# One step later for a copy, and a weight split moved into the first four tiles of a layer: a fused LSH-attention and mixture kernel

## The chip, the cores and the metric

The kernel runs on one core of one Trainium2 chip. The metric is the device time of one execution in microseconds (us), as the median over several runs. One of the executions was also recorded by the hardware profiler; every duration below comes from that recording.

## What is computed

The reference takes `q`, `k`, `v` of shape (2, 8, 768, 64): two batches, eight heads, 768 positions, 64 channels. Its core, with the hashing of rows to buckets in front of it, is:

```
mask   = q_bucket[:, :, :, None] == k_bucket[:, :, None, :]     # 6 sign bits of q @ proj and k @ proj
scores = where(mask, (q @ k^T) / 8, -1e9)
attn   = softmax(scores);  attn_out = attn @ v                   # (2, 8, 768, 64)
x      = attn_out laid out as (1536, 512)                        # heads side by side
out    = sum over 4 experts e of p[:, e] * (relu(x @ w1[e]) @ w2[e])
```

`w1` is (4, 512, 1024) and `w2` is (4, 1024, 512); `p` is the row-normalised `domain_probs`. All of it is held to the precision of float32, which the kernel reaches by splitting each operand into a rounded high part and a remainder ("hi" and "lo") and adding three products: hi times hi, hi times lo, lo times hi.

## The kernel before, in words

**Two batches, interleaved.** The attention of batch 0 runs first. Then the expert layers of batch 0 (function `moe`) run on TensorE while the attention of batch 1 is threaded between their tiles. Last come the expert layers of batch 1 (`moe_fast`). The order of all instructions is the program's own: each engine (TensorE = PE, VectorE = DVE, ScalarE = ACT, GpSimd = POOL, SyncE = SP, which issues all DMAs) takes its instructions strictly in the order in which the program writes them, and waits in place for whatever an instruction lacks. Buffers are freed by semaphores: a new tile in a pool with one buffer waits for the last reader of the old one, even where that reader is written later in the program, on another engine.

**The units of the expert layers.** There are 8 units per batch, one per half expert (512 hidden columns). In batch 0 a unit u has a first layer (lines 654 to 680: two halves s of 384 rows, four tiles f each, 12 matmuls per tile, lines 664 to 666) and a second layer (lines 620 to 643: six tiles t, 12 matmuls each, lines 627 to 629). ACT writes the rectified tile `hh` (line 671), DVE its remainder `hl` (line 672); for a second-layer tile DVE adds the result to `acc` (line 635). The tiles of PSUM for all of these rotate through four banks, which the attention's `ptps` and `pv` tiles share.

**The weights.** `load_w` (line 578) loads one 512 KB half of a weight matrix into one of two staging buffers `ws`. `split_w` (line 592) is a generator with four pieces per matrix: in a piece DVE casts 128x512 values to the high part (line 600) and POOL subtracts to get the low part (line 601); after pieces 2 and 4 the staging buffer is reloaded. The first weights of the next unit are split during the second layer, a piece after each of its first four tiles. The second-layer weights `w2hi`, `w2lo` of the unit are split during its own first layer, a piece whenever line 677 asks `sp2` for one. Before, that is after f = 1 and f = 3 of s = 0, and after f = 1 and f = 3 of s = 1. In the last unit of batch 0 (u = 7) the rest of the attention is written out before s = 1, and `x_ops` (lines 712 to 740), the preparation of the inputs of batch 1 on DVE, ACT and POOL, is written into s = 1.

**The attention as a pipeline.** `attention()` (line 502) runs over 96 steps i, one per head and tile of 128 rows; stage letters in the order "TXVSENRP" are written at each step, each for an earlier tile by its own lag. S computes scores on PE (lines 341, 343), DVE masks them, E is the exponential on ACT (line 364), N and R send reciprocals of the sums through memory (`row`, `rdb`), P prepares the next head. From head 9 on ("light") the transposed score tile of a pair of tiles, called a group g here, is made without PE:

```
elif op == "X":
    for lag, f in ((LAG_H, stage_h), (LAG_X, stage_x)):
        j = i - lag
        if 0 <= j < n and light(*seq[j][:2]) and j % G == G - 1:
            f(b, h, t // G)
```

`stage_x` (line 414, lag 3): DVE transposes 32x32 blocks into `t1`, SP writes `t1` to memory (`scr`, line 425), then reads it back rearranged into `px` with four DMAs (line 428). There is one `px` buffer. `stage_h` (line 434, `LAG_H`): for two halves, ACT copies `px` into the high part `pthi` (line 442), POOL forms `ptlo` (line 443). `stage_v` (line 447, lag 7): PE multiplies with v in two parts, part 0 with `pthi` at lag 7 and part 1 with `ptlo` at lag 8 (line 453). There are 21 such groups. Since j is odd, X(g+1) stands in the step in which H(g) stands before the change. How many steps of attention stand between two tiles of the expert layers is set by the numbers that the generators yield; neither edit changes one of these.

Of the kernel before, what the change touches and what calls it, by code (L numbers as in the profile page):

```python
# [39 lines left out]
LAG_VL = 7  # L40
DRAIN = 1000
LAG_X = 3
LAG_H = 5


@with_exitstack
def tile_lsh_attention__then__domain_moe(
# [454 lines left out]
    def attention():  # L502
# [3 lines left out]
        def do(op, i):  # L506
# [15 lines left out]
# [3 lines that stand above are left out]
# [67 lines left out]
    def split_w(g, i):  # L592
        n = ("w1", "w2")[i]
        hi = wp.tile([P, KD, HALF], F32R, tag=n + "hi", name=n + "hi")
        lo = wp.tile([P, KD, HALF], F32R, tag=n + "lo", name=n + "lo")
        wts[g, i] = (hi, lo)
        for c in range(0, KD, WC):
            t = staged.pop((g, i, c))
            for o in range(WC):
                nc.vector.tensor_copy(hi[:, c + o], t[:, o])  # L600
                nc.gpsimd.tensor_tensor(  # L601
                    out=lo[:, c + o], in0=t[:, o], in1=hi[:, c + o].bitcast(F32), op=ALU.subtract
                )
                if o == WC - 1:
                    load_w()
                yield
# [3 lines left out]
    def moe_ps():  # L610
        return one("mps")

    def second_layer(b, u, first_u, hs, w2):
        e = u // (F // HALF)
        nxt = first_u + u + 1
        w2hi, w2lo = w2
        more = nxt < B * NU
        fast = nxt >= NU
        sp = (split_w1_fast(nxt) if fast else split_w(nxt, 0)) if more else iter(())
        for s in range(NS - 1, -1, -1) if b else range(NS):  # L620
            for t in range(TS):
                tt = s * TS + t
                ts = slice(t * P, (t + 1) * P)
                ps = moe_ps()
                for f in range(FC):
                    hh, hl = hs[s, f]
                    nc.tensor.matmul(ps, hh[:, ts], w2hi[:, f], start=f == 0, stop=False)  # L627
                    nc.tensor.matmul(ps, hh[:, ts], w2lo[:, f], start=False, stop=False)  # L628
                    nc.tensor.matmul(ps, hl[:, ts], w2hi[:, f], start=False, stop=f == FC - 1)  # L629
                pcol = pe[:, b, tt, e : e + 1]  # L630
                if u == 0:
                    accs[b, tt] = ap_.tile([P, DM], F32, tag=f"acc{tt}", name="acc")
                    nc.vector.tensor_scalar(out=accs[b, tt], in0=ps, scalar1=pcol, scalar2=None, op0=ALU.mult)
                else:
                    nc.vector.scalar_tensor_tensor(  # L635
                        out=accs[b, tt], in0=ps, scalar=pcol, in1=accs[b, tt], op0=ALU.mult, op1=ALU.add
                    )
                if u == NU - 1:
                    nc.sync.dma_start(
                        out=out[b * S : (b + 1) * S, :].rearrange("(p c) d -> c p d", c=NT)[tt], in_=accs[b, tt]  # L640
                    )
                next(sp, 0)
                yield 2600
        for _ in sp:
            pass

    def moe(b, first_u):
        for u in range(NU):
            w1hi, w1lo = wts.pop((first_u + u, 0))
            sp2 = split_w(first_u + u, 1) if first_u + u else iter(())  # L650
            hs = {}
            nxt = first_u + u + 1
            xo = None
            for s in range(NS):
                if nxt == NU and s == 1:
                    while next(att, None) is not None:
                        pass
                    xo = x_ops()
                sl = slice(s * SB, (s + 1) * SB)
                for f in range(FC):  # L660
                    fs = slice(f * P, (f + 1) * P)
                    ps = moe_ps()
                    for kk in range(KD):
                        nc.tensor.matmul(ps[:, :SB], w1hi[:, kk, fs], xhi[b, kk][:, sl], start=kk == 0, stop=False)  # L664
                        nc.tensor.matmul(ps[:, :SB], w1hi[:, kk, fs], xlo[b, kk][:, sl], start=False, stop=False)  # L665
                        nc.tensor.matmul(  # L666
                            ps[:, :SB], w1lo[:, kk, fs], xhi[b, kk][:, sl], start=False, stop=kk == KD - 1
                        )
                    hh = hp.tile([P, SB], F32R, tag=f"hh{f}", name="hh")
                    hl = hp.tile([P, SB], F32R, tag=f"hl{f}", name="hl")  # L670
                    nc.scalar.activation(hh, ps[:, :SB], ACTF.Relu)  # L671
                    nc.vector.scalar_tensor_tensor(  # L672
                        out=hl, in0=ps[:, :SB], scalar=0.0, in1=hh.bitcast(F32), op0=ALU.max, op1=ALU.subtract
                    )
                    hs[s, f] = (hh, hl)
                    if f % 2 == 1:
                        next(sp2, 0)
                    yield 1960
                    if xo is not None and (s, f) >= (1, 1):
                        next(xo, 0)  # L680
            for _ in xo or ():
                pass
            yield from second_layer(b, u, first_u, hs, wts.pop((first_u + u, 1)))
# [28 lines left out]
    def x_ops():  # L712
        pair_in("b11", ((xp, "xe0"),))
        pair_in("t1", ((xp, "xe1"),))
        t1 = combine(b12, b11, ALU.subtract)
        put_hi("b11", b11)
        put_hi("t1", t1)
        put_lo("b11", b11, nc.gpsimd)
        put_lo("t1", t1, nc.gpsimd)
        pair_in("b21", ((stk, "q1"), (stk, "al")))  # L720
        pair_in("b22", ((stk, "q1"), (stk, "al")))
        pair_in("t2", ((stk, "ah"), (stk, "k2")))
        pair_in("t3", ((stk, "ah"), (stk, "k2")))
        pair_in("t4", ((ex, "t1"),))
        t2 = combine(b22, t1, ALU.subtract)
        put_hi("b21", b21)
        t4 = combine(t2, b21, ALU.subtract)
        put_hi("t2", t2)
        put_lo("b21", b21, nc.gpsimd)
        yield  # L730
        t3 = combine(b22, b12, ALU.subtract)
        put_lo("t2", t2, nc.vector)
        put_hi("b22", b22)
        put_hi("t4", t4)
        put_lo("b22", b22, nc.gpsimd)
        yield
        put_hi("t3", t3)
        put_lo("t4", t4, nc.vector)
        put_lo("t3", t3, nc.gpsimd)
        yield  # L740
# [135 lines left out]
    with tc.manual_schedule():  # L876
# [25 lines left out]
        for b in range(B):  # L902
            dm = da = 0.0
            for c in (moe_fast if b else moe)(b, b * NU):
                dm += c
                while da < dm * ATT_PACE * n_att / n_moe:
                    x = next(att, None)
                    if x is None:
                        break
                    da += x  # L910
            if b == 0:
                for _ in att:
                    pass
# [28 lines left out]
```

## Time and profile before

| | us |
|---|---|
| median of 3 runs (784.24 to 785.15) | 784.28 |
| the profiled execution, its time | 785.92 |
| its span, first to last instruction | 784.2 |
| PE busy in the span | 743.6 |
| DVE, ACT, POOL busy | 507.0, 362.1, 339.8 |

How to read it: the profiled execution's time is 1.7 us longer than its span, and 1.6 us longer than the median. PE is busy in 95% of the span, and no other engine in more than 65%. Busy time of matmuls is modelled and overlaps, so the distance between starts is the surer measure of what a matmul costs. The granted clock of PE has two levels, 1.2 and 2.4 GHz, shown as 0.5 and 1.0.

### The profile page before, as it was taken

What the parts mean: (1) busy time and instruction counts of PE and PEld (TensorE: products, weight loads), DVE (VectorE), ACT (ScalarE), POOL (GpSimd) and SP (SyncE); (2) the same over time, 40 slices, a digit from 0 to 9 for tenths busy, and PEclk for the clock granted to TensorE, in tenths of its full rate; (3) what the DMA queues carried; (4) which work ended last, traced back from release to release, by engine and by line L of the source; (5) the groups of instructions that cost most, each with busy time, mean ns of one, the idle gap of its engine ahead of it and who ended that gap; (6) DMA issues with size and microseconds to landing.
All of it is one profiled execution on the core that took longest, in us unless ns stands there. A gap on an engine that the chain in (4) does not pass through costs nothing. (4 is left out here: it accounts for less than half of the span.)

```text
span 784.2 us, 11424 instructions
## 1 busy us (share of the span) xinstructions
PE 743.6 (95%) x4090; PEld 673.4 (86%) x4090; DVE 507.0 (65%) x957; ACT 362.1 (46%) x731; POOL 339.8 (43%) x290
## 2 busy tenths in 40 slices
PE   7899999998999979999998999789999999999998
PEld 5889989996988969989897898669889889898896
DVE  5799999945565557655755433766585675765853
ACT  5899999742434343625345130414343352343430
POOL 1232442613466446554665552653342342433420
PEclk9999999999999989999998999989999999999999
DMA  4544644433767666667756612041130212211302
GB/s 101 150 107 117 141 98 115 113 93 117 215 191 216 187 183 199 185 210 193 217 182 192 200 39 80 28 147 68 54 101 34 81 55 81 81 54 54 101 8 80
DMA packets 71953, 95.49 MB, mean 122 GB/s; under 512 B 31396, under 2 KB 47268, under 8 KB 71896
## 3 DMA queue, kind: packets, MB, share of 16 engines
q1 hardware_dynamic: 71896, 94.76, 41.7%
q8 instruction: 32, 0.52, 0.3%
q14 instruction: 25, 0.20, 0.1%
HBM read 62.68 MB, written 19.71 MB: 105 GB/s over the span
## 5 line engine op out<-in xcount | busy, mean ns | idle before, releaser
L627 PE MATMUL mps<-w2hi,hh 128*128 128x512 f32 x384 | 153.4, 399 | 15.9 <-DVE w2hi L600 12.4
L628 PE MATMUL mps<-w2lo,hh 128*128 128x512 f32 x384 | 152.1, 396 | 3.9 <-POOL w2lo L601 3.9
L629 PE MATMUL mps<-w2hi,hl 128*128 128x512 f32 x384 | 152.2, 396 | 0.0
L635 DVE SCALAR_TENSOR_TENSOR acc<-mps,pe,acc 128x512 f32<-128x512 f32 x84 | 62.8, 748 | 78.1 <-PE mps L629 77.1
L443 POOL TENSOR_TENSOR ptlo<-px,pthi 128x768 fp32r<-128x768 f32 x42 | 77.1, 1856 | 61.6 <-ACT pthi L442 60.9
L627 PEld LDWEIGHTS mps<-w2hi,hh 128*128 128x128 f32 x384 | 72.9, 190 | 33.9 <-issue 8.1
L803 POOL TENSOR_TENSOR w2lo<-ws,w2hi 128x512 fp32r<-128x512 f32 x32 | 45.8, 1452 | 120.3 <-ACT w2hi L802 120.3
L348 DVE TENSOR_SCALAR_CACHE_REDUCE p<-sps 128x768 f32<-128x768 f32 x96 | 90.7, 945 | 4.8 <-PE sps L343 4.4
L664 PE MATMUL mps<-xs,w1hi 128*128 128x384 f32 x256 | 87.8, 343 | 3.9 <-DVE hl L672 3.9
L672 DVE SCALAR_TENSOR_TENSOR hl<-mps,hh 128x384 fp32r<-128x384 f32 x64 | 35.6, 556 | 86.1 <-ACT hh L671 85.8
L364 ACT ACTIVATE p<-p,nb 128x768 f32<-128x768 f32 x96 | 89.5, 932 | 2.4 <-DVE p L348 1.8
L628 PEld LDWEIGHTS mps<-w2lo,hh 128*128 128x128 f32 x384 | 73.1, 190 | 20.1 <-POOL w2lo L601 6.6
L629 PEld LDWEIGHTS mps<-w2hi,hl 128*128 128x128 f32 x384 | 73.0, 190 | 17.6 <-DVE hl L832 2.4
L666 PE MATMUL mps<-xs,w1lo 128*128 128x384 f32 x256 | 86.8, 339 | 0.0
L665 PE MATMUL mps<-xs,w1hi 128*128 128x384 f32 x256 | 86.8, 339 | 0.0
L442 ACT ACTIVATE pthi<-px 128x768 fp32r<-128x768 f32 x42 | 33.2, 838 | 97.5 <-DMA px<-scr 97.5
L671 ACT ACTIVATE hh<-mps 128x384 fp32r<-128x384 f32 x64 | 30.9, 488 | 81.3 <-PE mps L666 81.1
L601 POOL TENSOR_TENSOR w1lo<-ws,w1hi 128x512 fp32r<-128x512 f32 x32 | 41.6, 1302 | 60.1 <-DVE w1hi L600 45.5
L601 POOL TENSOR_TENSOR w2lo<-ws,w2hi 128x512 fp32r<-128x512 f32 x32 | 42.4, 1329 | 50.5 <-DVE w2hi L600 26.0
L409 DVE TENSOR_TENSOR ptlo<-ptps,pthi 128x384 fp32r<-128x384 f32 x108 | 54.6, 547 | 8.4 <-ACT pthi L408 8.1
L343 PE MATMUL sps<-k,al 76*128 76x384 f32 x192 | 50.6, 344 | 3.6 <-POOL vv L302 2.6
L341 PE MATMUL sps<-ah,q 128*128 128x384 f32 x192 | 50.9, 345 | 2.3 <-DVE p L348 0.9
(134 smaller groups left out, 1567.4 us busy)
## 6 DMA issues: line engine op xcount, KB each, us to landing
ws<-in_moe_w_dram SPq DMA_DIRECT2D x64, 512.0 KB
scr<-t SPq DMA_DIRECT2D x21, 768.0 KB
px<-scr SPq DMA_DIRECT2D x84, 192.0 KB
q<-ah SPq DMA_DIRECT2D x30, 192.0 KB
tv<-in_v_dram SPq DMA_DIRECT2D x16, 192.0 KB
rdb<-row SPq DMA_DIRECT2D x48, 64.0 KB
out_dram<-acc SPq DMA_DIRECT2D x12, 256.0 KB
tqk<-in_q_dram SPq DMA_DIRECT2D x15, 192.0 KB
```

Source lines behind the costliest of these rows:

```text
L348: nc.vector.tensor_scalar(out=two(pt), in0=ps[:, :, :NH], scalar1=MASKED, scalar2=MASKED, op0=ALU.min, op1=ALU.min, accum_out=nb,)
L364: nc.scalar.activation(pt, pt, ACTF.Exp, bias=nb, scale=-1.0, accum_out=dens[b, h, g][:, o : o + 1])
L409: nc.vector.tensor_tensor(out=ol, in0=src, in1=oh.bitcast(F32), op=ALU.subtract)
L443: nc.gpsimd.tensor_tensor(out=fl[:, sl], in0=px[:, sl], in1=fh[:, sl].bitcast(F32), op=ALU.subtract)
L601: nc.gpsimd.tensor_tensor(out=lo[:, c + o], in0=t[:, o], in1=hi[:, c + o].bitcast(F32), op=ALU.subtract)
L627: nc.tensor.matmul(ps, hh[:, ts], w2hi[:, f], start=f == 0, stop=False)
L628: nc.tensor.matmul(ps, hh[:, ts], w2lo[:, f], start=False, stop=False)
L629: nc.tensor.matmul(ps, hl[:, ts], w2hi[:, f], start=False, stop=f == FC - 1)
L635: nc.vector.scalar_tensor_tensor(out=accs[b, tt], in0=ps, scalar=pcol, in1=accs[b, tt], op0=ALU.mult, op1=ALU.add)
L664: nc.tensor.matmul(ps[:, :SB], w1hi[:, kk, fs], xhi[b, kk][:, sl], start=kk == 0, stop=False)
L665: nc.tensor.matmul(ps[:, :SB], w1hi[:, kk, fs], xlo[b, kk][:, sl], start=False, stop=False)
L666: nc.tensor.matmul(ps[:, :SB], w1lo[:, kk, fs], xhi[b, kk][:, sl], start=False, stop=kk == KD - 1)
```

## The change

Two edits. The lag of `stage_h` goes from 5 to 6 steps: ACT's copy of `px` and POOL's subtraction are written one attention step later, after the X of the next group instead of before it, and one step before the first matmul that reads `pthi` instead of two. And a piece of the split of `w2` is written after each of the four tiles of s = 0, none in s = 1. The reload of the staging buffers moves with the pieces. It holds for units 1 to 7 of batch 0; unit 0's `w2` is split earlier, and `moe_fast` has its own split.

```diff
-LAG_H = 5
+LAG_H = 6
...
                     hs[s, f] = (hh, hl)
-                    if f % 2 == 1:
+                    if s == 0:
                         next(sp2, 0)
                     yield 1960
```

## Rows read from the trace of the kernel before

**Rows 1.** The page, busy time by engine (us, share of the span, instructions).
```profile
PE 743.6 (95%) x4090; PEld 673.4 (86%) x4090; DVE 507.0 (65%) x957; ACT 362.1 (46%) x731; POOL 339.8 (43%) x290
```

**Rows 2.** Busy time by stage, PE alone: stretch, length, busy, granted clock, DMA share, GB/s.
```profile
273.32:303.95 30.63, 25.49 (x122) 0.89 0.70 196
...
400.00:429.01 29.01, 25.60 (x140) 0.88 0.56 166
...
501.89:529.24 27.35, 18.58 (x73) 0.81 0.33 105
...
543.90:560.55 16.65, 16.65 (x73) 1.00 0.29 95
```

**Rows 3.** Who waited for whom, PE: total us, times, longest.
```profile
PE mps L627 <- DVE w2hi L600: 12.4, 3, 7.6
PE mps L628 <- POOL w2lo L601: 3.9, 5, 1.1
...
PE hps L275 <- DVE al L264: 3.1, 5, 1.5
```

**Rows 4.** Timeline, unit 7, end of first layer: start, length, engine, what, [idle before].
```profile
502.23 2.50 DVE L706 TENSOR_TENSOR xc<-xc,xraw 128x768 f32<-128x768 f32 x1
...
510.08 1.55 DVE L600 CAST w2hi<-ws 128x512 fp32r<-128x512 f32 x1
...
511.78 0.76 PE L627 MATMUL mps<-w2hi,hh 128*128 128x512 f32 x1 [7.64 <-DVE w2hi L600]
```

**Rows 5.** Timeline, PE, second layer of unit 2.
```profile
275.23 0.39 PE L629 MATMUL mps<-w2hi,hl 128*128 128x512 f32 x1
280.20 0.80 PE L627 MATMUL mps<-w2hi,hh 128*128 128x512 f32 x1 [4.59 <-DVE w2hi L600]
...
284.85 0.39 PE L627 MATMUL mps<-w2hi,hh 128*128 128x512 f32 x1
```

**Rows 6.** Timeline, ACT and DVE, the same stretch of unit 2.
```profile
275.37 1.58 ACT L442 ACTIVATE pthi<-px 128x768 fp32r<-128x768 f32 x2 [6.67 <-DMA px<-scr]
...
277.36 0.56 DVE L672 SCALAR_TENSOR_TENSOR hl<-mps,hh 128x384 fp32r<-128x384 f32 x1 [6.58 <-ACT hh L671]
...
279.18 0.97 DVE L600 CAST w2hi<-ws 128x512 fp32r<-128x512 f32 x1
```

**Rows 7.** Timeline, ACT and PE, first layer of unit 5.
```profile
415.97 1.57 ACT L442 ACTIVATE pthi<-px 128x768 fp32r<-128x768 f32 x2 [7.10 <-DMA px<-scr]
...
418.56 0.69 PE L664 MATMUL mps<-xs,w1hi 128*128 128x384 f32 x1 [3.41 <-DVE hl L672]
...
422.57 1.49 PE L453 MATMUL pv<-pthi,vv 128*128 128x256 f32 x6
```

**Rows 8.** Who waited for whom, ACT and SP, stretch 186 to 455.
```profile
ACT pthi L442 <- DMA px<-scr: 97.5, 18, 11.8
...
SPq L428 <- DMA scr<-t: 77.1, 21, 6.3
...
SPq L428 <- POOL ptlo L443: 0.9, 2, 0.8
```

**Rows 9.** Timeline, the DMA queue of SP, groups 4 and 5.
```profile
240.38 1.75 SPq L428 DMA_DIRECT2D px<-scr  x4
...
257.03 1.76 SPq L428 DMA_DIRECT2D px<-scr  x4
```

**Rows 10.** Timeline, ACT and POOL, group 5.
```profile
262.65 1.58 ACT L442 ACTIVATE pthi<-px 128x768 fp32r<-128x768 f32 x2 [3.13 <-DMA px<-scr]
...
263.58 3.84 POOL L443 TENSOR_TENSOR ptlo<-px,pthi 128x768 fp32r<-128x768 f32 x2 [5.41 <-ACT pthi L442]
```

**Rows 11.** Timeline, PE, the product with v: group 3 part 1, group 4 part 1, group 5 part 0.
```profile
252.27 0.88 PE L453 MATMUL pv<-ptlo,vv 128*128 128x256 f32 x6
...
261.45 0.88 PE L453 MATMUL pv<-ptlo,vv 128*128 128x256 f32 x6
...
267.10 0.88 PE L453 MATMUL pv<-pthi,vv 128*128 128x256 f32 x6
```

## The prediction

> **What bounds the kernel now.** I read the page first: PE is busy in 95% of the span, no other engine in more than 65% [rows 1]. So the time can fall only by what PE idles, or runs at its lower clock, and those have to be found stage by stage. The view of busy time by stage, cut at the starts of the first and second layers, shows where: the second layers of batch 1 take 16.65 us with PE never idle at the full clock, while three stages of batch 0 stand out by idle time and a granted clock under 1.00: the second layer of unit 2, the first of unit 5 and the second of unit 7 [rows 2]. The list of waits then names what ended the idle time: `w2hi` three times for 12.4 us in all, `w2lo` five times for 3.9, the head preparation's `al` [rows 3], and in unit 5 `hl`, 3.41 at once [rows 7].
>
> The timelines show why each was late. In unit 7 the fourth `w2hi` cast is the last thing on DVE behind `x_ops`, whose additions take up to 2.50; it ends at 511.6, and PE has waited 7.64 for it [rows 4]. In unit 2 the fourth cast stands behind `hl`, `hl` behind `hh`, and ACT could not do `hh` because it sat 6.67 us in front of `pthi`, waiting for `px` to land [rows 6]. Unit 5 is the same chain without the cast: ACT idle 7.10 for `px`, so `hh` and `hl` late, so no free PSUM bank [rows 7]. ACT spends 97.5 us, in 18 waits, at that instruction [rows 8]. Most of it cost PE nothing.
>
> Behind `px` stands SP: every `px` read waited for `scr` to land, 77.1 us in 21 waits, and only 0.9 us for POOL's `ptlo` to free the single `px` buffer [rows 8]. I expect that balance to turn.
>
> **Part one, the split of w2.** It removes and adds no instruction: 28 casts, 28 subtractions and 14 reloads in seven units stand earlier, in unit 7 before `x_ops`.
> - *Unit 7.* The stage takes 27.35 and the undisturbed one 16.65 [rows 2]: 10.7 us, with the half clock after the stall in it. What is late next is DVE: `x_ops` without the cast ends near 511, then come the six additions to `acc` and the mixes for batch 1. PE without the stall reaches its fifth tile at 501.9 + 4 x 2.78 = 513.0 (16.65 / 6 for a tile), when the first tile's bank has to be free, about 512.5 by DVE's queue. It fits without margin. I take 10.7 and keep 7 as the low end.
> - *Unit 2.* From 275.23 to 284.85 is 9.62 us [rows 5]. The work in it at full clock is four steps of 0.23 within the layer (16.65 / 72), 0.7 for six products with v and 0.7 for the scores: about 2.4. So 7.2 us, unless the layer is late for another reason.
> - *`w2lo`.* The waits of 0.85, 0.84 and 0.56 in units 1, 5 and 6 are inside the 3.9 [rows 3]; the fourth subtraction now ends four tiles before it is read. 2.2 us.
> - *Its cost.* The casts need weights that have landed three tiles earlier. The tightest is unit 5: SP's timeline has its second half issued at 399.4, 0.6 us before the unit starts at 400.0 [rows 2]; the piece is wanted after the third tile, about 407 to 408. A `px` read of 768 KB lands 5.6 us after its first issue (257.03 to ACT's start at 262.65) [rows 9, 10], so I put these 512 KB at 405. Nothing, at most 1 us of DVE, covered by the PSUM banks.
>
> **Part two, the copy a step later.** The gain is unit 5: at 418.56 the stall of 3.4 ends, the tile then takes 4.01 at half clock, 2.0 more than at full, and about 0.9 follows in the product with v [rows 7]: 6.3 us. The head preparation's 1.5 us [rows 3] stands behind the same ACT wait. With unit 2 above, the two parts free 10.7 + 7.2 + 2.2 + 6.3 + 1.5 = 27.9 us.
>
> The cost is in the loop of `px`. Every DMA behind a `px` read on SP waits with it: the `row`, `rdb` and next `scr` of the groups, the head preparation's moves and loads, the weight loads. Before, H(g) stood ahead of X(g+1) in the same step; now it stands one step behind it, so `px`(g+1) cannot be issued before ACT has reached the next step, copied, and POOL has subtracted. Call P the start of part 1 of group g-1, the first PE work of the step in which H(g) now stands. ACT reaches H about 1.9 us after P (an estimate from these groups' mean durations: `hh` 0.49, the exponential 0.93 and its two small followers 0.5). POOL's pair ends 4.8 us after ACT's copy begins (262.65 to 267.42) [rows 10]. So `px`(g+1) is issued at P + 6.7 at the soonest and lands at P + 12.3, while the next P comes about 12 later. In an ordinary pair of steps that is just in time: ACT waits little, PE not at all, since part 0 is read 5.7 after P (261.45 to 267.10) [rows 11] and the copy is done by P + 3.5.
>
> But in the loop where a head is prepared SP needs more: from `px` of group 4 to `px` of group 5 it took 16.65 [rows 9]; the move and load issues of the preparation lie in between. Before, group 4 was 11.9 ahead of its P (240.38 against 252.27) [rows 9, 11], a reserve that took this up. Now that reserve is capped near 12 - 6.7 = 5.3. Worked for group 5: `px`(4) at about 244.4 instead of 240.4, `px`(5) at 244.4 + 16.65 = 261.0, landed 266.7, copied by 268.3; PE wants it at 267.10 less the 0.85 already won: 266.2. A new stall of 2.1 us. Five such loops lie in the 21 groups (groups 2, 5, 8, 11, 14). The same steps give 0 to 2.7 at these and 0 to 2 at the ordinary groups after the last of them, because PE, rid of its old stalls, is then close behind SP. I take ten us in all. Bounds: 0, if SP's queue shortens by what it waited in vain, and 20, if the five loops each cost 4 us (16.65 less 12). Stalls this short need not pull the clock down: by the view of stages, unit 4's wait of 1.5 left it at 1.00.
>
> **The sum.** 27.9 - 10 = 17.9 us. The profiled execution's 785.92 becomes 768.0; it stands 1.6 above the median of the runs, so the median becomes 784.28 - 17.9, about 766.
>
> **The rivals.**
> - *The loop hides.* SP keeps up, and all 27.9 come out: 756. For it: SP's loops of 10 to 12 us without a preparation. Against: the head loop of 16.65.
> - *The loop eats the attention's gain.* The stalls of 7.2, 6.3 and 1.5 return as waits for `pthi`; what stays is unit 7 and `w2lo`, 12.9 us: 771, or up to 775 if DVE gives back 4 in unit 7.
> - *Slower.* The wait for `pthi` becomes the rule. If ACT comes to H not 1.9 but some 6 us after P, the copy ends at P + 7.6, 1.9 after PE wants it, in each of 20 groups: 38 us against 27.9, so 794. It decides from 1.4 us a group. For it: the thin margin of 2.2 us; against: ACT is busy in 46% of the span and, rid of the wait at the old place, has nothing to be late with.
> - *DVE and POOL in each other's way.* The cast took 0.97 and 1.55 with POOL at work beside it [rows 4, 6], and an addition of `x_ops` 2.50. If DVE's queue in unit 7, rid of one cast, is still stretched by POOL, now at `x_ops` without a pause, the second layer ends with DVE near 522 instead of 518.5, and 3.5 of the 17.9 are given back: 770. The Trainium skill, "SBUF — State Buffer", section "Who interferes with whom", says that a VectorE cast and GpSimd want one shared port pair, and that whoever is second is blocked for the other's whole instruction; by that the additions stay long here too, and the trace agrees in those durations.
>
> **Chances.** The forecast 0.50 (its own range 760 to 770), the loop hides 0.17, the loop eats the gain 0.15, DVE and POOL 0.08, slower 0.07; 0.03 that these cancel to no change. A measurement of this kernel can tell about 0.2%, 1.6 us. Faster 0.90, same 0.03, slower 0.07. From 755 to 775 leaves out the slower cases and the tails.
>
> **What would show it.** Right: no PE wait for `w2hi` in units 1 to 7, unit 7's second layer at 17 to 20 us; no stall on `hl` in unit 5; ACT's 97.5 us at `pthi` cut to under half; SP's wait for `ptlo` at the `px` read grown from 0.9 to tens of us, and PE waits for `pthi` of 1 to 3 us in head loops, some 10 in all. Wrong: `pthi` waits over 28 us in sum or followed by the half clock, or unit 7 still over 25 us.

## The result, and the profile after

The changed kernel takes 774.73 us (median of 4 runs, 774.09 to 776.73) against 784.26 of the kernel before: a ratio of 0.9881, 95% interval 0.9861 to 0.9901. It is faster by 9.5 us. The prediction said 766 with a range of 755 to 775, so the time lies at the very edge of the range, and where the forecast saw 17.9 us about half of that came.

The page after, busy time by engine. PE executes the same 4090 instructions and is busy for 741.1 us instead of 743.6 [rows 1]; the span is 11 us shorter:

```profile
span 773.0 us, 11420 instructions
...
PE 741.1 (96%) x4090; PEld 672.6 (87%) x4090; DVE 514.1 (67%) x957; ACT 363.8 (47%) x731; POOL 340.8 (44%) x290
```

Busy time by stage, PE alone (stretch, length, busy, granted clock, DMA share, GB/s): the first layer of unit 2, the second of unit 2, the first of unit 3, the second of unit 4, the first of unit 5, the second of unit 7; and, from the same view, units 1 to 5 with nothing left out.

```profile
247.55:274.58 27.03, 25.08 (x143) 0.94 0.74 213
274.58:297.93 23.35, 23.35 (x122) 1.00 0.77 215
297.93:328.88 30.95, 26.19 (x145) 0.89 0.61 177
...
376.39:404.14 27.75, 23.67 (x118) 1.00 0.58 182
404.14:428.10 23.96, 22.98 (x140) 1.00 0.63 193
...
500.38:517.97 17.59, 17.02 (x73) 1.00 0.09 34
...
201.52:448.45 246.93, 233.13 (x1266) 0.98 0.67 194
```

The same stretch of units 1 to 5 before:

```profile
202.49:449.11 246.62, 233.98 (x1266) 0.97 0.68 197
```

The three stages of [rows 2] are mended: unit 2's second layer fell from 30.63 to 23.35, unit 5's first from 29.01 to 23.96, unit 7's second from 27.35 to 17.59. But units 1 to 5 as a whole take 246.93 instead of 246.62. Other stages have become long: the first layer of unit 2 is now 27.03, the first of unit 3 is 30.95, at a clock of 0.89, and the second of unit 4 is 27.75. The same three before:

```profile
250.16:273.32 23.16, 23.16 (x144) 1.00 0.68 191
...
303.95:327.66 23.71, 23.71 (x145) 1.00 0.62 188
...
376.91:400.00 23.09, 23.09 (x119) 1.00 0.69 205
```

So in units 1 to 5 the change as a whole gained nothing, and unit 7's 9.8 us are the result.

What PE waits for has changed hands. The list of waits after (engine, line, total us, times, longest), to be set beside [rows 3]:

```profile
PE pv L453 <- ACT pthi L442: 9.8, 5, 4.2
PE pv L453 <- POOL ptlo L443: 3.9, 3, 1.9
PE mps L627 <- DVE acc L633: 3.5, 1, 3.5
PE hps L275 <- DVE al L264: 2.2, 6, 0.7
```

`w2hi` and `w2lo` are gone from it; before, `pthi` had one wait of 0.64 and `ptlo` none. SP and ACT in the stretch 186 to 455, to be set beside [rows 8]:

```profile
SPq L428 <- DMA scr<-t: 78.6, 21, 6.2
SPq L387 <- DMA row<-rt: 40.4, 18, 3.9
SPq L428 <- POOL ptlo L443: 11.7, 11, 1.8
...
ACT pthi L442 <- DMA px<-scr: 54.7, 13, 9.3
```

ACT's wait for `px` fell from 97.5 to 54.7, and SP's wait for `ptlo` before a `px` read rose from 0.9 in 2 to 11.7 in 11.

One head loop shows how these hang together. SP's queue, groups 4 and 5, to be set beside [rows 9]:

```profile
242.33 2.87 SPq L428 DMA_DIRECT2D px<-scr  x4
...
253.33 0.75 SPq L425 DMA_DIRECT2D scr<-t  x1
260.93 1.76 SPq L428 DMA_DIRECT2D px<-scr  x4
```

ACT and POOL in the same loop, to be set beside [rows 10]:

```profile
251.65 1.57 ACT L442 ACTIVATE pthi<-px 128x768 fp32r<-128x768 f32 x2
...
266.49 1.58 ACT L442 ACTIVATE pthi<-px 128x768 fp32r<-128x768 f32 x2 [5.70 <-DMA px<-scr]
...
256.25 0.91 POOL L281 TENSOR_SCALAR al<-k,bit_mul 44x768 fp32r<-44x768 f32 x1 [3.54 <-DMA ah<-al]
257.24 3.66 POOL L443 TENSOR_TENSOR ptlo<-px,pthi 128x768 fp32r<-128x768 f32 x2
```

And PE, the product with v, group 4 part 1 and group 5 part 0, to be set beside [rows 11], then the longest wait of all, group 8 part 0:

```profile
260.96 0.98 PE L453 MATMUL pv<-ptlo,vv 128*128 128x256 f32 x6 [1.95 <-POOL ptlo L443]
268.25 0.89 PE L453 MATMUL pv<-pthi,vv 128*128 128x256 f32 x6
...
308.76 1.65 PE L453 MATMUL pv<-pthi,vv 128*128 128x256 f32 x6 [4.21 <-ACT pthi L442]
```

ACT finished group 4's copy at 253.2, yet POOL began `ptlo` only at 257.24. One step later means one place further back in POOL's queue too: the head preparation's `al` (line 281) now stands in front, and it waited 3.54 for the move of `ah`, a DMA that stands behind the `px` read in SP's queue. So `px` of group 5 left at 260.93, 18.6 after that of group 4 instead of 16.65, and both PE and SP waited for the same `ptlo`. In the head loops of groups 5, 8, 11 and 14 alike, `ptlo` begins 5.6 to 7.3 us after ACT's copy does; in [rows 10] it was 0.9.

### The profile page after: what moved, and what is told of

The parts are those of the page before. It is cut to its first block, busy times and chain, and to the rows that moved or that the text cites. A ratio compares the mean times of both kernels' runs of the same rounds, so it can differ in the third digit from the quotient of the medians.

```text
span 773.0 us, 11420 instructions
## 1 busy us (share of the span) xinstructions
PE 741.1 (96%) x4090; PEld 672.6 (87%) x4090; DVE 514.1 (67%) x957; ACT 363.8 (47%) x731; POOL 340.8 (44%) x290
## 4 chain that ended last, share of the span: by engine, by line
PE 70%; DMA 10%; DVE 10%; ACT 3%; POOL 3%; issue 2%; SPq 1%; POOLq 0%; ACTq 0%; DVEq 0%
PE mps L627 9%; PE mps L629 9%; PE mps L628 9%; PE pv L453 5%; PE mps L664 4%; PE mps L666 4%; PE mps L665 4%; DMA px<-scr 3%; DMA scr<-t 3%; DVE p L348 3%; PE ptps L404 2%; PE hps L275 2%; PE sps L343 2%; PE mps L821 2%; PE mps L817 2%; PE mps L820 2%
## 5 line engine op out<-in xcount | busy, mean ns | idle before, releaser
L628 PE MATMUL mps<-w2lo,hh 128*128 128x512 f32 x384 | 150.4, 392 | 0.0
L442 ACT ACTIVATE pthi<-px 128x768 fp32r<-128x768 f32 x42 | 33.1, 836 | 55.9 <-DMA px<-scr 54.7
L453 PE MATMUL pv<-pthi,vv 128*128 128x256 f32 x288 | 45.8, 295 | 9.9 <-ACT pthi L442 9.8
L281 POOL TENSOR_SCALAR al<-k,bit_mul 44x768 fp32r<-44x768 f32 x15 | 13.7, 913 | 93.2 <-DMA ah<-al 55.0
```

The lines of the kernel that those rows point to most:

```text
L453: nc.tensor.matmul(ps[:, :GN].rearrange("p (a q) -> p a q", q=32) if light(b, h) else ps[:, :GN], vv[:, c], pts[b, h, g][part][:, c], star ...
```

## The experiments

Each run has its own runs of the kernel before beside it, on the same chip; these gave medians of 786.6 (e1 to e4), 788.3 (e5 to e7) and 787.6 (e8, e9), so across these groups the ratios are to be compared, not the times. The column for units 1 to 5 is the stretch from the start of unit 1's first layer to the start of unit 6's first, and the next the second layer of unit 7, both from the profiled execution.

| run | split early | lag | other | median us | ratio to before, 95% | units 1 to 5 | unit 7, 2nd |
|---|---|---|---|---|---|---|---|
| before | no | 5 | | 784.26 | 1 | 246.6 | 27.4 |
| after | yes | 6 | | 774.73 | 0.9881 (0.9861 to 0.9901) | 246.9 | 17.6 |
| e1 | yes | 5 | | 765.52 | 0.9732 (0.9683 to 0.9781) | 236.1 | 17.6 |
| e2 | no | 6 | | 796.54 | 1.0126 (1.0068 to 1.0184) | 258.9 | 27.4 |
| e3 | unit 7 alone | 5 | | 775.26 | 0.9857 (0.9810 to 0.9904) | 246.3 | 17.6 |
| e4 | yes | 6 | two px | 765.62 | 0.9728 (0.9678 to 0.9778) | 234.8 | 17.6 |
| e5 | yes | 6 | rdb later | 773.44 | 0.9814 (0.9782 to 0.9845) | 244.3 | 17.6 |
| e6 | yes | 5 | rdb later | 767.71 | 0.9723 (0.9691 to 0.9755) | 238.2 | 17.6 |
| e7 | yes | 6 | two px, rdb later | 756.05 | 0.9591 (0.9569 to 0.9614) | 226.8 | 17.6 |
| e8 | yes | 5 | two px, rdb later | 758.06 | 0.9613 (0.9566 to 0.9659) | 230.8 | 17.6 |
| e9 | no | 6 | two px, rdb later | 769.93 | 0.9773 (0.9725 to 0.9820) | 230.3 | 28.1 |

**e1, the early split alone** (after, with one line back):

```diff
-LAG_H = 6
+LAG_H = 5
```

> Only the split of w2 early; the copy stays at lag 5. Theory A (the single px buffer: the copy a step later makes the next px read wait for ptlo, and that hands the attention's gain back): nothing is handed back here, units 2 and 7 and the w2lo waits come out, unit 5's stall of 6.3 us stays: 784.3 - 10 - 7 - 2 = 765 us, at most 768. Theory B (SP's own loop of scr, px, row and rdb sets the pace of batch 1's attention, whatever the lag): the stalls of units 1 to 6 return elsewhere, only unit 7's is gone: 774 us, within 2.

It came to 765.52, as theory A had it; theory B's 774 is out. Waits of the px read in that run, SP and ACT, stretch 186 to 455:

```profile
SPq L428 <- DMA scr<-t: 74.1, 21, 4.3
...
ACT pthi L442 <- DMA px<-scr: 92.7, 17, 8.1
```

ACT stands at `pthi` for 92.7 us again, and the kernel is still 1.5% faster than with both edits. So that wait is cheap.

**e2, the copy a step later alone** (before, with one line changed):

```diff
-LAG_H = 5
+LAG_H = 6
```

> Only the copy a step later; the split of w2 stays. Both theories keep the 7.6 us wait in unit 7. Theory A: some 15 us won in units 2, 4 and 5 and some 15 lost to px: 784 us, with ptlo named at the px read for over 10 us. Theory B: the same 784 us, since the pace is SP's. A third view, that ACT freed of its wait is worth something by itself: 775 us or less.

It is slower than before, 1.0126, which neither theory had: I had thought the stalls it removes would pay for those it makes. Its waits, PE first, then SP:

```profile
PE pv L453 <- ACT pthi L442: 11.1, 5, 4.3
PE mps L627 <- DVE w2hi L600: 7.6, 1, 7.6
PE mps L628 <- POOL w2lo L601: 4.8, 3, 3.1
...
PE pv L453 <- POOL ptlo L443: 2.8, 1, 2.8
```

```profile
SPq L428 <- POOL ptlo L443: 18.2, 12, 4.0
```

The four cells before, e1, e2 and after add up to within 1.5 us in units 1 to 5: the early split takes 10.5 us off with lag 5 (246.6 to 236.1) and 12.0 with lag 6 (258.9 to 246.9); the later copy costs 12.3 without the split and 10.8 with it.

**e3, the early split in unit 7 alone:**

```diff
-                    if f % 2 == 1:
+                    if (s == 0) if u == NU - 1 else (f % 2 == 1):
```

> The early split in unit 7 alone, the copy at lag 5. All theories: unit 7's second layer near 17.5 us, and 784.3 - 9.8 = 774.5 us. If so, everything else in the change sums to nothing; if it is above 778, the early split in units 1 to 6 or the lag has a gain of its own.

775.26, and unit 7's second layer 17.6. That one unit gives as much as the whole change. Units 1 to 5 are there the same program as before, and take 246.3 against 246.6: in this one pair two profiled executions agree to 0.3 us.

**e4, both edits and px in two buffers.** The second buffer is one that stands empty until unit 7, so nothing else gives up room:

```diff
-        px = ex.tile([P, G, S], F32, tag="pt", name="px")
+        odd_px = (h * NT // G + g) % 2
+        px = (xp if odd_px else ex).tile([P, G, S], F32, tag="xe0" if odd_px else "pt", name="px")
```

> Both edits, and px in two buffers in turn, so that the px read of the next group need not wait for ptlo. Theory A: that wait was the price, so it goes to 0 at the px read and the 15 us handed back come out: 760 us, at most 764. Theory B: the wait for ptlo goes and the loop is as long as before, for it was SP's: 772 to 775 us.

765.62, theory A's direction at somewhat less than its size. SP's wait for `ptlo` falls from 11.7 to 0.2, and units 1 to 5 fall by 12.1 us. The single buffer was the larger part of the price. PE still waits 5.5 us for `pthi` there, and ACT 30.4 for `px`: something else is still late. SP, PE, and units 1 to 5 in e4 (its extra line moves the line numbers by one):

```profile
SPq L429 <- POOL ptlo L444: 0.2, 1, 0.2
...
PE pv L454 <- ACT pthi L443: 5.5, 3, 2.3
...
202.95:437.74 234.79, 229.28 (x1265) 0.99 0.70 204
```

**e5, e6 and e7, the read of `rdb` a step later.** One line, in after (e5), in e1 (e6) and in e4 (e7):

```diff
-LAG_R = 4
+LAG_R = 5
```

> Both edits, and the rdb read written one attention step later (lag 5 instead of 4), behind the next px read, so that SP no longer stands waiting for the row write to land (40 us in 18 waits with both edits) before it comes to the next scr. If the length of SP's own loop makes pthi late (16.7 us in the loops that prepare a head, against 12 of PE's), PE's 14 us of waits for pthi and ptlo fall by half or more: 767 us. If the single px buffer alone does it, the wait only moves to ptlo at the px read, 11.7 us becoming 30, and the time stays: 772 to 775 us.

> The early split alone (copy at lag 5) with the rdb read a step later. What is left of stalls with the early split alone is 6.6 us of PE idle in units 2 to 5, on hl and p, behind ACT's 92.7 us at pthi. If SP's loop makes px late there, ACT's wait falls under 60 us and the stalls go: 757 to 760 us, the best of all. If those stalls have another cause, 765 us.

> Both edits, px in two buffers, the rdb read a step later: neither the buffer nor the row write holds SP. The 5.5 us of PE waits for pthi that two buffers left go: 757 to 760 us. If the copy a step later has a price of its own, beyond the buffer, it stays at 765 us, above the early split alone with the later rdb.

In e5 SP's wait for the row write fell from 40.4 to 1.6, but units 1 to 5 only from 246.9 to 244.3, and the ratio from 0.9881 to 0.9814: most of the wait moved on, to `ptlo` and to `scr`. SP in e5:

```profile
SPq L428 <- DMA scr<-t: 90.3, 20, 6.6
SPq L428 <- POOL ptlo L443: 25.9, 16, 3.3
...
SPq L387 <- DMA row<-rt: 1.6, 1, 1.6
```

In e6 it gave nothing, the second of the two cases expected: ratio 0.9723 beside e1's 0.9732, and ACT still waits 95.4 for `px`. With one buffer the way round from `px` to `ptlo` is the limit, and SP's other waits hide in it (SP's wait for `ptlo` is 11.3 there, 0.6 in e1). In e7, with the buffer doubled first, the same line is worth 8.0 us in units 1 to 5 (234.8 to 226.8), and the kernel takes 756.05, 32.3 us less than its own runs of before. Busy time by stage in e7, units 3 and 4, then units 1 to 5:

```profile
295.06:318.86 23.80, 23.79 (x145) 1.00 0.74 216
318.86:341.74 22.88, 22.88 (x118) 1.00 0.67 200
341.74:365.24 23.50, 23.50 (x145) 1.00 0.84 248
365.24:388.12 22.88, 22.88 (x118) 1.00 0.65 187
...
202.52:429.30 226.78, 226.77 (x1266) 1.00 0.74 213
```

PE is idle for 0.01 us in 226.78, at the full clock throughout. This is the floor of that part, for the matmuls as they are, and the others can be measured against it: before stood 19.8 us above it, after 20.1, the early split alone 9.3.

**e8 and e9, the freed loop with one edit each.** e8 is e7 with `LAG_H = 5`; e9 is e7 with the old condition `if f % 2 == 1`.

> The same freed loop (px in two buffers, rdb a step later) with the early split, but the copy at lag 5. If the copy a step later is worth something once its price is paid, this stays near 766 us, ten above the run with lag 6, with some 90 us of ACT waits at pthi and PE stalls on hl, p or al. If the freed loop alone did it and the lag is worth nothing, 756 to 758 us.

> The freed loop with the copy at lag 6 and the old split. Only what hangs on the late casts comes back: unit 7's 10 us and the w2lo waits of 2 to 4 us, while unit 2, whose fourth cast was late through ACT's wait, stays clean: 756 + 12 = 768 us. If unit 2's stall needs the early split, 775 us.

e8 came to 758.06: the freed loop does nearly all of what e7 gains on e1. The later copy is then worth 4 us in units 1 to 5 of the profiled executions (230.8 to 226.8); but the one of e8 was the slowest of its four runs and the one of e7 the fastest, and the intervals of the two ratios overlap, so the whole-kernel gain is not settled. e9 came to 769.93, near the 768 expected. Unit 7 is back at 28.1, while unit 2's second layer stays clean with the late casts (23.5 us from 272.0 on). PE's waits in e9:

```profile
PE mps L628 <- DVE w2hi L601: 8.0, 2, 7.6
...
PE mps L629 <- POOL w2lo L602: 3.0, 3, 1.3
```

(Here too the extra line moves the line numbers by one.)

## Why the prediction came out as it did, step by step

- **Unit 7, 10.7 with a low end of 7.** Right: 9.8 in the stage, and e3 shows that it stands alone. The four casts take 0.42 each there, at 487 to 494, ahead of `x_ops`. The warning that it fits without margin was right as well: the fifth tile just finds its bank free, and PE waits 0.3 for `acc` before the sixth.
- **Unit 2, `w2lo`, unit 5, unit 4: 17.2 in all.** Right as to the places: each of those stalls is gone. Their sum is of the right size too: e7, which pays nothing for it, has 19.8 us less in units 1 to 5 than before, against 15.0 from units 2, 4 and 5 and 1.7 from `w2lo` there. It has two edits more, though, and no run shows what those give without the change.
- **The price of the later copy, 10 us, bounds 0 to 20.** This is the term that was mis-sized. It measures 20.1 after, against the floor of e7: the upper bound, which was itself rounded down, since five times 16.65 less 12 is 23. Of the 20.1, 13.8 are idle time of PE, and 6.4 are matmuls that took longer (busy 233.1 us against 226.8). Set against the early split alone, the later copy was forecast to lose 10 less its gains of 6.3 and 1.5, that is 2.2; it lost 10.8. The mechanism was right, and e4 shows it for the larger part: with the buffer wait, 12.1 of the 20.1 go. That the worked example came close is luck, for two misses cancelled: `px` of group 4 left at 242.33 and not at 244.4, the loop then took 18.6 and not 16.65, and so `px` of group 5 left at 260.93 where 261.0 was forecast. The stall of about 2 us came, but at `ptlo` of group 4; at `pthi` of group 5, where it was forecast, PE did not wait. What the sum left out is in the rows above. First, POOL: I let `ptlo` follow the copy at once, P + 6.7, and did not look at what stands between the old and the new place in POOL's queue. The head preparation's `al` does, and it waits for a DMA. Group 4's `ptlo` ended 7.7 us after its copy, not 3.2 (253.2 to 260.9; in the rows of before 264.2 to 267.4). Second, the clock: I put it at nothing for stalls this short, and one was 4.2 us; the matmuls after it ran at half the clock (0.89 over that stage). The ordinary groups were in the sum, at 0 to 2 each: of PE's eight waits for `pthi` or `ptlo`, 13.7 us, three are there, 4.7 us.
- **Its own signs.** Of the signs of being right, three came: no wait for `w2hi` in units 1 to 7, unit 7's second layer between 17 and 20, no stall on `hl` in unit 5. Two came only in part: ACT's wait at `pthi` did not fall to under half of 97.5 (54.7), and SP's for `ptlo` grew to 11.7, barely the "tens". And one sign of being wrong came: the `pthi` wait of 4.21 was followed by the half clock.
- **The rivals.** "The loop eats the attention's gain" is nearest to what came: 771 to 775 forecast, 774.7 measured; it had a chance of 0.15. Its upper end was to come from DVE, which should give back 4 in unit 7; that stage is only 0.9 over the undisturbed 16.65, and the loop took back all of the 19.8. That the time still lies in the range is luck too: with 27.9 freed and 20.1 paid it would be 776.5, outside; the gains were larger as well, 19.8 and 9.8. "Slower" has the sign of e2, 1.0126, but not its mechanism: ACT came to group 4's copy 2.0 us after P (249.67 to 251.65), not 6. "The loop hides" is nearest to e7, which needed two edits more and gains 32.3, not 27.9. "DVE and POOL" did not decide: the additions of `x_ops` stayed at 2.42 and 2.50 beside POOL's subtractions (the one that began just before POOL's first, at 497.42, took 0.95), but unit 7's stage is 17.6, not 20. The Trainium skill, "SBUF — State Buffer", section "Who interferes with whom", says that a VectorE instruction with two inputs in SBUF contends with a GpSimd instruction that reads SBUF; those durations agree.
- **Left open.** Why e4 alone and e1 alone come to the same 765.5 by different stalls, and how much of e8's last 4 us is DMA order: not tried.

The additions of `x_ops` after, DVE, end of the first layer of unit 7, with the fourth cast ahead of them, to be set beside [rows 4]:

```profile
493.26 0.42 DVE L600 CAST w2hi<-ws 128x512 fp32r<-128x512 f32 x1
...
498.47 2.42 DVE L706 TENSOR_TENSOR xc<-xraw,xc 128x768 f32<-128x768 f32 x1
500.93 2.50 DVE L706 TENSOR_TENSOR xc<-xc,xraw 128x768 f32<-128x768 f32 x1
```

## What to carry to other kernels

A long wait on an engine off the critical path (97.5 us of ACT here) is not by itself a cost (92.7 of it stayed in a kernel 21 us faster); before moving the instruction that waits, ask who is released by it. With one buffer, the reader's place in the program is also the next writer's, and moving the reader to a later place lengthens the loop, holds every DMA queued behind that write, and can put the reader behind other work on its engines, as POOL's `al` here. Where a change mixes two edits, measure each alone: here one gave some 20 us and the other took 11 of them back, until a second buffer and a later read of `rdb` removed its price.

## What the runs showed of the hardware that was not expected

Waits of PE of about the same length were not always followed by the lower clock. After the change, the first layer of unit 2 has one wait of 1.95 us and a mean clock of 0.94, while the second layer of unit 4 has two, 1.40 and 2.55, and keeps 1.00. With the early split alone, 2.10 us in unit 3 came with 0.94 and 2.01 in unit 5 with 1.00, as these rows of PE's timeline and of busy time by stage show:

```profile
315.68 0.45 PE L664 MATMUL mps<-xs,w1hi 128*128 128x384 f32 x1 [2.10 <-DVE hl L672]
...
412.34 0.44 PE L664 MATMUL mps<-xs,w1hi 128*128 128x384 f32 x1 [2.01 <-DVE hl L672]
...
298.66:326.07 27.41, 25.31 (x145) 0.94 0.71 210
...
395.33:420.41 25.08, 23.07 (x139) 1.00 0.69 206
```

Against the same stages of e7 (23.80 and 22.59) the first is 3.6 us longer and the second 2.5: so a stall of some 2 us cost once 1.5 us more than its own length, and once 0.5. What makes the difference is not shown.
